# Two FF slices of six chunks moved into the attention stage, with partial sums kept in DRAM

## The chip, the cores and the metric

The kernel runs on one core of one Trainium2 chip. The time is that of one execution in device microseconds. Three runs of the kernel before gave 1572.54, 1577.17 and 1578.33 us, with a median of 1577.17 us.

## The reference

Three layers follow each other, all in float32 (4608 tokens of 512 features):

```python
# 1. attention, 8 batches x 8 heads, 576 queries, 64 features; keys and values pooled by 8 to 72
scores = scale * np.matmul(q, k_p.transpose(0, 1, 3, 2)); attn = softmax(scores); x = attn @ v_p
# 2. gated feed-forward, FF = 1536
g = x @ w_gate; x = (g * sigmoid(g) * (x @ w_val)) @ w_out
# 3. top-1 expert of 8 (width 1024), chosen by logits = x @ w_gate2 + bias[modality]
out[mask] = gate_w[mask, None] * (np.maximum(x[mask] @ w1[e], 0) @ w2[e])
```

## The kernel before

**Stage 1, attention.** 36 tiles of up to 128 queries (`steps`; five per pair of batches hold both heads' halves of a remainder). For a tile x, `st_scores` makes the scores on TensorE and the exponentials on ScalarE, `st_norm` sums and normalises (VectorE and GpSimd), `st_aT` transposes, and `st_av` multiplies by the pooled values and writes x transposed to DRAM (`xT_d`, by a DMA from ScalarE's queue, L313). The pieces are not written in the order of the loop: each is entered with a key by `at_key` (scores of tile x at x-3.0, normalising at x-1.7, transposing at x, and so on; loads and the first weights have keys too) and the pieces are then emitted sorted by key. One key is one tile. The emission order is a priority: a planner, working ahead of the run with durations of its own, fixes the order on each engine, and may take a ready instruction that is emitted somewhat later. At run time each engine, SP's DMA queue among them, works through its own list strictly in order.

**Splits.** All products of stages 2 and 3 are made from two rounded halves (hi, lo), three matmuls for each product: hi·hi, hi·lo and lo·hi. `w_split` makes the halves of one weight part (gate, value or out of one FF slice of 128; three parts a slice): one ScalarE pass, four VectorE passes (L137 to L142), one copy and one subtraction (L149, L150). Weights come as 64-bit numbers, so each part is a DMA of 512 KB (`w_load`). The parts of the first two slices (0 to 5) have keys 21 to 33.5 in the attention; the others follow during stage 2. `x_load` reads one chunk of x (384 tokens) in four pieces through two buffers (`xr`), and splits each (L186 on ScalarE, L187 on VectorE); chunks 0 and 1 have keys 27 and 30.

**Stage 2, feed-forward.** 12 chunks of 384 tokens, 12 slices each: an item (c, f) is `gemm1` (24 matmuls 128x384, line L372, then tanh and products on ScalarE and VectorE) and `gemm2` (9 matmuls 128x512, L394, which add into three PSUM banks over all 12 slices of the chunk). The items of chunks 0 and 1 alternate for as long as weights are split, then chunks 2 to 11 run one after the other. At the end of a chunk `evac` (L403, ScalarE) takes the sums into `row` tiles; `logits` and `gates` (queued in `todo`, one for each item) make the choice of expert, and the rows go to DRAM (`x2_d`).

**Stage 3, experts**, in blocks of 256 gathered tokens: `e_gemm1` (12 matmuls 128x256, L665) and `e_gemm2` (6 matmuls 128x512, L684) for each of 8 slices. The change does not touch it except for the order in which token tiles are numbered.

PSUM has eight banks in one pool for the whole kernel: tag s 2 (`st_av`, `gemm1`), tag x 4 (scores, then sums), tag y 2 (transposes, then sums). `gemm1` of chunk 0 therefore shares its two banks with `st_av`.

Of the kernel before, what the change touches and what calls it, by code (L numbers as in the profile page):

```python
# [44 lines left out]
def const_array():  # L45
    import numpy as np

    p = np.arange(128)
    parts = {"ident": np.eye(128)}
    vm = np.zeros((128, 4, 2, 2))  # L50
    for r in range(H * KEYS):
        c, row, h = r // 128, r % 128, r // KEYS
        vm[row, h // 2, c - h // 2, h % 2] = 1.0 / 8
    parts["vmask"] = vm.reshape(128, 16)
    parts["idhi"] = np.tile(np.arange(TILES) * 1.0, (128, 1))
# [11 lines left out]
def attention_moe_moe2(ctx: ExitStack, tc: tile.TileContext, q, k, v, w_gate, w_val, w_out,  # L67
# [8 lines left out]
    psp = ctx.enter_context(tc.tile_pool(name="psp", bufs=1, space=PSUM))  # L76

    def bank(tag, name):
        return psp.tile([128, 512], F32, tag=tag, bufs={"s": 2, "x": 4, "y": 2}[tag], name=name)

    xT_d = [dram.tile([128, 4, 2 * S], F32, name=f"xT{g}") for g in range(4)]
    x2_d = dram.tile([NT + 1, DM + 1], F32, name="x2d")


    ncst = sum(w for _, w in CONST_W)
# [66 lines left out]
    def load_bias(p0):  # L152
        t0 = m1.tile([128, 2, CH], F32, tag="xh", bufs=4, name="biast").rearrange("p a n -> p (a n)")
        mraw = t0[:TILES, 0:256].bitcast(I32).rearrange("i (p w) -> i p w", w=2)
        mf = t0[:TILES, 256:384]
        m = t0[:, 384:420]
        z = t0[:, 420:456]
        tmp = t0[:, 456:744].rearrange("p (t e) -> p t e", e=E)
        bb = t0[:, 744:760].rearrange("p (m e) -> p m e", e=E)
        sy.dma_start(out=mraw.rearrange("i p w -> i (p w)"),  # L160
                     in_=modality.bitcast(I32).rearrange("(i x) -> i x", i=TILES))
        sy.dma_start(out=bb.rearrange("p m e -> p (m e)"),
                     in_=mbias.rearrange("m e -> (m e)").partition_broadcast(128))
        ve.tensor_copy(mf, mraw[:, :, 0])
        mps = bank("s", "mps")
# [24 lines left out]
        xc[c] = (hi, lo)  # L190


    w2p = [None]
    with tc.tile_pool(name="p0", bufs=1) as p0:
# [52 lines left out]
        def st_scores(x):  # L247
            b, i = steps[x]
            e = e_t[x % NE]
            nm = p0.tile([128, 8], F32, tag="nm", bufs=4, name="nm")  # L250
            for j in range(2):
                sc = bank("x", "sc")
                for hp in (2 * j, 2 * j + 1):
                    dst = sc[:, (hp % 2) * 144:(hp % 2) * 144 + 144]
                    if i < 4:
                        pe.matmul(dst, lhsT=q_t[b][:, hp, i * 128:(i + 1) * 128],
                                  rhs=kb_t[b % 2][:, hp].rearrange("p r k -> p (r k)"), start=True, stop=True)
                    else:
# [24 lines left out]
        def st_aT(x):  # L283
# [4 lines left out]
            else:  # L288
                views = [(b + w, 1, slice(64 * w, 64 * w + 64), slice(256, 320)) for w in range(2)]
            for c0, cn in ((0, 4), (4, 1)):  # L290
                ap = bank("y", "aTp")[:, 0:cn * 128].rearrange("p (c n) -> p c n", c=cn)
                for c in range(cn):
                    pe.transpose(ap[:, c, :], e[:, (c0 + c) * 128:(c0 + c + 1) * 128], ident)
                for bb, half, ss, cs in views:
                    o = at_tile(bb, half)[:, c0:c0 + cn, cs]
                    if cn == 1 or x % 2:
                        ve.tensor_copy(o, ap[:, :, ss])  # L297
                    else:
                        ac.copy(o, ap[:, :, ss])

        def st_av(b, half, hp):
# [16 lines left out]
            ev_.append((key, len(ev_), fn, args))  # L318

        as_, an, av, avs = 3.0, 1.7, 0.7, 0.45  # L320
        for x in range(len(steps)):
            at_key(x - as_, st_scores, x)
            at_key(x - an, st_norm, x)
# [61 lines left out]
    def gemm2(c, f):  # L385
        hh, hl = h_t.pop((c, f))
        w = wo[f // 2]
        if f == 0:
            x2ps[c] = [bank("xxy"[tt], "x2") for tt in range(CT)]
        for tt in range(CT):  # L390
            o = x2ps[c][tt]
            ts = slice(tt * 128, (tt + 1) * 128)
            for n, (a, hx) in enumerate(((0, hh), (1, hh), (0, hl))):
                pe.matmul(o, lhsT=hx[:, ts], rhs=w[:, f % 2, a, :], start=f == 0 and n == 0,  # L394
                          stop=f == NF - 1 and n == 2)

    rows_t, small = {}, {}

    def evac(c):
        rows = []  # L400
        for tt in range(CT):
            r = m1.tile([128, DM + 1], F32, tag="row", bufs=3, name="row")
            ac.activation(out=r[:, 0:DM], in_=x2ps[c][tt], func=ACTF.Copy, scale=0.5)  # L403
            rows.append(r)
        rows_t[c] = rows
# [420 lines left out]
```

## Time and profile before

| | us |
|---|---|
| median of three runs | 1577.17 |
| the profiled execution's own time | 1575.83 |
| its span (first to last instruction) | 1574.1 |
| stage 1: start to the first `gemm1` matmul (L372) | 192.3 |
| stage 2: from there to its last matmul, some | 907 |
| TensorE busy over the span | 1505.1 (96%) |
| VectorE, ScalarE, GpSimd busy | 949.3, 617.1, 194.5 |

The profile names engines PE (TensorE), PEld (its weight loads), DVE (VectorE), ACT (ScalarE), POOL (GpSimd) and SP. A wait is told by the engine that idles and the instruction that ended the wait. Matmuls are pipelined, so a duration in a row overlaps the next one; the pace is read from the starts.

### The profile page before, as it was taken

Reading aid. Unit: us, or ns where it says so; the run is one execution under the profiler, and the core shown is the slowest. Engines: PE = TensorE matmul, PEld = TensorE weight load, DVE = VectorE, ACT = ScalarE, POOL = GpSimd, SP = SyncE. Lnnn points to the kernel's source line nnn. Section 1 sums busy time; section 2 is a strip of 40 time slices with the busy share of each in tenths; the row PEclk is TensorE's granted clock in tenths of the full one; section 3 lists DMA queues with packets and bytes.
Section 4 is the critical chain, followed back from the end, with each engine's and each line's share of the span. In section 5 each row is a group of like instructions: output and inputs, shape, how many; then the busy total and the mean of one; then the engine's idle time right before and its main releaser. Section 6 shows DMA issues by size and latency. Waiting matters only on the chain.

```text
span 1574.1 us, 22647 instructions
## 1 busy us (share of the span) xinstructions
PE 1505.1 (96%) x8472; PEld 1367.7 (87%) x8472; DVE 949.3 (60%) x2252; ACT 617.1 (39%) x1385; POOL 194.5 (12%) x201
## 2 busy tenths in 40 slices
PE   5778899999999999999999999999999999999996
PEld 4566699999999999999999999998889889898985
DVE  5677799555555564637272727277986666666660
ACT  4567555432222121212121212123556656666661
POOL 4866300000000000000000000001031111211101
PEclk8998999999999999999999999999999999999998
DMA  7775534210000000000010100007477666666520
GB/s 287 291 268 187 184 139 161 67 31 30 11 30 31 11 31 31 11 30 24 17 41 1 40 1 31 1 21 265 141 231 258 224 229 223 218 225 224 191 98 28
DMA packets 47816, 179.58 MB, mean 114 GB/s; under 512 B 5421, under 2 KB 19921, under 8 KB 34898
## 3 DMA queue, kind: packets, MB, share of 16 engines
q1 hardware_dynamic: 33170, 149.19, 26.9%
q0 software_dynamic: 6080, 19.42, 3.5%
q10 hardware_dynamic: 8448, 9.44, 1.7%
q8 instruction: 68, 1.11, 0.3%
q14 instruction: 50, 0.41, 0.1%
HBM read 149.70 MB, written 28.86 MB: 113 GB/s over the span
## 4 chain that ended last, share of the span: by engine, by line
PE 85%; DVE 4%; issue 4%; POOL 4%; DMA 2%; ACT 1%; POOLq 0%; SPq 0%; ACTq 0%
PE gv L372 38%; PE x L394 19%; PE hp L665 12%; PE po L684 12%; PE xp L308 2%; POOL vraw L232 1%; PE tp L649 1%; POOL e L276 1%; DVE kp L222 1%; DMA x2d<-row 1%; ACT e L267 1%; DVE sm L273 1%; DVE at L297 0%; POOL vb L238 0%; DVE nm L263 0%
## 5 line engine op out<-in xcount | busy, mean ns | idle before, releaser
L372 PE MATMUL gv<-xh,gv 128*128 128x384 f32 x2304 | 611.3, 336 | 0.2 <-DVE t L377 0.2
L372 PEld LDWEIGHTS gv<-xh,gv 128*128 128x128 f32 x2304 | 421.1, 188 | 6.8 <-DVE t L377 0.6
L372 PE MATMUL gv<-xl,gv 128*128 128x384 f32 x1152 | 390.4, 339 | 0.0
L394 PE MATMUL x<-wo,hh 128*128 128x512 f32 x864 | 273.4, 398 | 0.0
L665 PEld LDWEIGHTS hp<-x2hl,w 128*128 128x128 f32 x1824 | 234.1, 189 | 10.9
L665 PE MATMUL hp<-x2hl,w 128*128 128x256 f32 x1824 | 243.1, 282 | 0.0
L372 PEld LDWEIGHTS gv<-xl,gv 128*128 128x128 f32 x1152 | 216.3, 188 | 5.9
L377 DVE SCALAR_TENSOR_TENSOR t<-t,gv 128x384 f32<-128x384 f32 x144 | 79.6, 552 | 233.1 <-ACT t L376 232.6
L376 ACT ACTIVATE t<-gv 128x384 f32<-128x384 f32 x144 | 70.7, 491 | 327.0 <-PE gv L372 326.7
L684 PE MATMUL po<-w,hh 128*128 128x512 f32 x608 | 193.4, 400 | 3.1 <-ACT hh L669 3.1
L414 DVE CUSTOM_DVE_ANT_0 junk<-row,w2g 128x512 bf16<-128x512 f32 x288 | 184.8, 684 | 3.6 <-ACT row L403 3.5
L394 PEld LDWEIGHTS x<-wo,hh 128*128 128x128 f32 x864 | 161.6, 189 | 27.0
L636 DVE TENSOR_TENSOR w<-raw,w 128x512 fp32r<-128x512 f32 x152 | 106.1, 698 | 116.8 <-ACT w L634 116.6
L381 ACT CAST hh<-t 128x384 fp32r<-128x384 f32 x144 | 73.8, 513 | 258.6 <-DVE t L378 258.4
L394 PE MATMUL x<-wo,hl 128*128 128x512 f32 x432 | 171.2, 396 | 0.0
L559 POOL DMA_INDIRECT xg<-x2d,gidx x38 | 38.3, 1007 | 1052.0 <-DVE oidx L546 913.2
L634 ACT CAST w<-raw 128x512 fp32r<-128x512 f32 x152 | 94.0, 619 | 135.4 <-PE po L684 124.8
L378 DVE TENSOR_TENSOR t<-t,gv 128x384 f32<-128x384 f32 x144 | 79.3, 551 | 74.3 <-PE gv L372 74.1
L684 PE MATMUL po<-w,hl 128*128 128x512 f32 x304 | 121.4, 399 | 0.0
L684 PEld LDWEIGHTS po<-w,hh 128*128 128x128 f32 x608 | 103.7, 188 | 17.6 <-ACT hh L669 3.3
L382 DVE TENSOR_TENSOR hl<-t,hh 128x384 fp32r<-128x384 f32 x144 | 80.1, 556 | 51.8 <-ACT hh L381 51.5
L638 DVE TENSOR_TENSOR w<-raw,w 128x512 fp32r<-128x512 f32 x152 | 103.7, 682 | 0.0
(127 smaller groups left out, 1468.8 us busy)
## 6 DMA issues: line engine op xcount, KB each, us to landing
raw<-in_moe_w_dram SPq DMA_DIRECT2D x76, 1024.0 KB, 4.9
vraw<-in_v_dram SPq DMA_DIRECT2D x8, 1280.0 KB, 12.0
x2d<-row SPq DMA_DIRECT2D x36, 256.5 KB, 3.7
kraw<-in_k_dram SPq DMA_DIRECT2D x8, 1152.0 KB, 8.8
qt<-in_q_dram SPq DMA_DIRECT2D x8, 1152.0 KB, 7.0
xr<-xT SPq DMA_DIRECT2D x48, 192.0 KB, 2.4
w2g<-in_moe_w_gate_dram SPq DMA_DIRECT2D x12, 512.0 KB, 3.6
w2g<-in_moe_w_val_dram SPq DMA_DIRECT2D x12, 512.0 KB, 3.5
```

The lines of the kernel that those rows point to most:

```text
L372: pe.matmul(p, lhsT=w[:, a, ws], rhs=x[kk], start=n == 0, stop=n == 11)
L377: ve.scalar_tensor_tensor(out=t, in0=t, scalar=1.0, in1=o[0], op0=ALU.add, op1=ALU.mult)
L378: ve.tensor_tensor(out=t, in0=t, in1=o[1], op=ALU.mult)
L381: ac.copy(hh, t)
L382: ve.tensor_tensor(out=hl, in0=t, in1=hh.bitcast(F32), op=ALU.subtract)
L394: pe.matmul(o, lhsT=hx[:, ts], rhs=w[:, f % 2, a, :], start=f == 0 and n == 0, stop=f == NF - 1 and n == 2)
L414: ve.tensor_tensor_reduce(out=junk, in0=r[:, 0:DM], in1=w2g[:, e, :], scale=1.0, scalar=0.0, op0=ALU.mult, op1=ALU.add, accum_out=L[:, tt, ...
L634: ac.copy(h1, src)
L636: ve.tensor_tensor(out=w[:, 1, 0:512].rearrange("p (k f) -> p k f", k=4), in0=src, in1=h1.bitcast(F32), op=ALU.subtract)
L638: ve.tensor_tensor(out=w[:, 1, 512:1024], in0=w2s, in1=w[:, 0, 512:1024].bitcast(F32), op=ALU.subtract)
L665: pe.matmul(hp, lhsT=w[:, a, c0:c0 + 128], rhs=x[:, kk, :], start=n == 0, stop=n == 11)
L684: pe.matmul(b["po"][tt], lhsT=hx[:, ts], rhs=w[:, a, 512:1024], start=f == 0 and n == 0, stop=f == 7 and n == 2)
```

## The change

Tokens 0 to 2303 (chunks 0 to 5) are also cut into nine units of 256 tokens. FF slices 0 and 1 of these units are computed during stage 1: `u_load` (x of a unit, split), `u_gemm1` (24 matmuls 128x256 and the products) and `u_gemm2` (6 matmuls 128x512), entered with keys 7 to 33.85, one item (u, f) every 1.5 keys. The sums of both slices of a unit go through `row` tiles to DRAM (`part_d`). In stage 2 chunks 6 and 7 come first, with all 12 slices, then chunks 0 to 5 with slices 2 to 11 only, then 8 to 11. `new_rows` loads the partial sums of a chunk, and `evac` adds them on VectorE instead of copying on ScalarE. The splits of weight parts 0 to 5 move from keys 21 to 33.5 to keys 1 to 6, their loads likewise. Stage 1 has a PSUM pool of its own: scores 2 banks (4 before), transposes 2, `st_av` and `u_gemm1` together 2, unit sums 2.

```diff
+EC, EF = 6, 2
+NU = EC * CT // 2
+ORDER = [EC, EC + 1] + list(range(EC)) + list(range(EC + 2, NCH))
+POS = {c: i for i, c in enumerate(ORDER)}
...
-        return psp.tile([128, 512], F32, tag=tag, bufs={"s": 2, "x": 4, "y": 2}[tag], name=name)
+        n = {"s": 2, "x": 4, "y": 2, "sc": 2, "at": 2, "xg": 2, "acc": 2}[tag]
+        return psp[0].tile([128, 512], F32, tag=tag, bufs=n, name=name)
...
+    part_d = [dram.tile([CH, DM], F32, name=f"part{c}") for c in range(EC)]
...
+    def u_load(u):
+        hi, lo = [], []
+        for k2 in range(2):
+            th = m1.tile([128, 2, CH], F32R, tag="xh", bufs=4, name="uh")
+            tl = m1.tile([128, 2, CH], F32R, tag="xl", bufs=4, name="ul")
+            for j in range(2):
+                raw = m1.tile([128, CH], F32, tag="xr", bufs=2, name="ur")[:, 0:256]
...
+                    sy.dma_start(out=raw, in_=xT_d[g0][:, 2 * k2 + j, c0:c0 + 256])
...
+                ac.copy(h, raw)
+                ve.tensor_tensor(out=l, in0=raw, in1=h.bitcast(F32), op=ALU.subtract)
...
+    def u_gemm1(u, f):
+        hi, lo = ue[u]["x"]
+        w = wgv[f]
+        p = bank("xg", "ugv")
+        o = [p[:, 0:256], p[:, 256:512]]
...
+                    pe.matmul(o[j], lhsT=w[:, a, ws], rhs=x[kk], start=n == 0, stop=n == 11)
...
+        ac.activation(out=t, in_=o[0], func=ACTF.Tanh, scale=0.5)
+        ve.scalar_tensor_tensor(out=t, in0=t, scalar=1.0, in1=o[0], op0=ALU.add, op1=ALU.mult)
+        ve.tensor_tensor(out=t, in0=t, in1=o[1], op=ALU.mult)
...
+        ac.copy(hh, t)
+        ve.tensor_tensor(out=hl, in0=t, in1=hh.bitcast(F32), op=ALU.subtract)
...
+    def u_gemm2(u, f):
...
+            ue[u]["acc"] = [bank("acc", "acc") for _ in range(2)]
+        for tt in range(2):
+            for n, (a, hx) in enumerate(((0, hh), (1, hh), (0, hl))):
+                pe.matmul(ue[u]["acc"][tt], lhsT=hx[:, ts], rhs=w[:, f % 2, a, :], start=f == 0 and n == 0,
+                          stop=f == EF - 1 and n == 2)
+        if f == EF - 1:
+            for tt in range(2):
+                r = m1.tile([128, DM + 1], F32, tag="row", bufs=3, name="urow")[:, 0:DM]
+                ac.activation(out=r, in_=ue[u]["acc"][tt], func=ACTF.Copy, scale=0.5)
+                ac.dma_start(out=part_d[c][y * 128:(y + 1) * 128, :], in_=r)
...
-                sc = bank("x", "sc")
+                sc = bank("sc", "sc")
...
-            xp = bank("s", "xp")
+            xp = bank("xg", "xp")
...
+        WS0, WSK, U0, UK = 1.0, 1.0, 7.0, 1.5
-                at_key(12.0 + n, w_load, n)
-                at_key(21.0 + (n - 4) * 2.5 + 0.1, w_load, n)
+            at_key(WS0 - 2.5 + n * 0.5 if n < 4 else WS0 + (n - 4) * WSK + 0.1, w_load, n)
-            at_key(21.0 + n * 2.5, w_split, n)
+            at_key(WS0 + n * WSK, w_split, n)
+        uitems = [(u, f) for u in range(NU) for f in range(EF)]
+        for n, (u, f) in enumerate(uitems):
+            x = U0 + n * UK
+            if f == 0:
+                at_key(x - 3.0, u_load, u)
+            at_key(x, u_gemm1, u, f)
+            at_key(x + 0.9 * UK, u_gemm2, u, f)
-        at_key(5.0, load_bias, p0)
-        at_key(27.0, x_load, 0)
-        at_key(30.0, x_load, 1)
+        at_key(3.5, load_bias, p0)
+        at_key(31.0, x_load, ORDER[0])
+        at_key(34.5, x_load, ORDER[1])
...
+    psp[0] = ctx.enter_context(tc.tile_pool(name="psp", bufs=1, space=PSUM, reuse_waits="tile"))
...
+    def new_rows(c):
...
+                sy.dma_start(out=rows_t[c][tt][:, 0:DM], in_=part_d[c][tt * 128:(tt + 1) * 128, :])
...
     def evac(c):
...
+            if c < EC:
+                ve.scalar_tensor_tensor(out=r, in0=x2ps[c][tt], scalar=0.5, in1=r, op0=ALU.mult, op1=ALU.add)
+            else:
+                ac.activation(out=r, in_=x2ps[c][tt], func=ACTF.Copy, scale=0.5)
...
-    for c in range(2, NCH):
-        items += [(c, f) for f in range(NF)]
+    for c in ORDER[2:]:
+        items += [(c, f) for f in range(EF if c < EC else 0, NF)]
```

## Rows read from the trace of the kernel before

**Rows 1.** The page: span, and busy time of each engine
```profile
span 1574.1 us, 22647 instructions
PE 1505.1 (96%) x8472; PEld 1367.7 (87%) x8472; DVE 949.3 (60%) x2252; ACT 617.1 (39%) x1385; POOL 194.5 (12%) x201
```

**Rows 2.** Stretch, length; busy PE, PEld, DVE, ACT, POOL; PEclk, DMA share, GB/s
```profile
0.00:20.00 20.00, 8.33 (x37) 7.72 (x37) 9.99 (x17) 8.88 (x30) 3.56 (x15) 0.95 0.91 371
20.00:55.00 35.00, 25.36 (x126) 19.88 (x126) 21.07 (x47) 18.12 (x71) 27.00 (x26) 0.83 0.63 252
55.00:192.30 137.30, 110.94 (x597) 87.36 (x595) 103.70 (x211) 88.08 (x311) 83.86 (x85) 0.93 0.60 217
192.30:341.90 149.60, 149.39 (x785) 139.51 (x784) 110.56 (x222) 72.31 (x123) 0.00 (x0) 1.00 0.33 115
341.90:1099.10 757.20, 755.23 (x3989) 704.76 (x3987) 409.08 (x1136) 163.97 (x331) 3.09 (x3) 1.00 0.10 33
```

**Rows 3.** PE's waits up to 200 us: total, times, longest
```profile
PE aTp L293 <- POOL e L276: 28.3, 15, 4.4
PE xp L308 <- ACT xs L310: 5.5, 3, 2.4
```

**Rows 4.** PE in order of time: the first `gemm1` matmul of two neighbouring items
```profile
1003.16 0.34 PE L372 MATMUL gv<-xh,gv 128*128 128x384 f32 x1
...
1009.46 0.34 PE L372 MATMUL gv<-xh,gv 128*128 128x384 f32 x1
```

**Rows 5.** PE in order of time: one slice of an expert block
```profile
1301.19 1.57 PE L665 MATMUL hp<-x2hl,w 128*128 128x256 f32 x12
1302.59 0.63 PE L684 MATMUL po<-w,hh 128*128 128x512 f32 x2
...
1304.01 1.57 PE L665 MATMUL hp<-x2hl,w 128*128 128x256 f32 x12
```

**Rows 6.** Groups of DVE instructions by line and shape, 0 to 192.3 us
```profile
L140 DVE SCALAR_TENSOR_TENSOR wa<-w2g,wa 128x512 int32<-128x512 int32 x9 | 8.7, 962 | 0.2
L142 DVE SCALAR_TENSOR_TENSOR wa<-w2g,wa 128x512 int32<-128x512 int32 x9 | 7.4, 826 | 0.1
L138 DVE TENSOR_SCALAR wa<-wa 128x512 int32<-128x512 int32 x9 | 5.3, 590 | 0.1
L137 DVE TENSOR_SCALAR wa<-wa 128x512 f32<-128x512 f32 x9 | 4.9, 541 | 0.4 <-ACT wa L136 0.4
L150 DVE TENSOR_TENSOR gv<-wa,gv 128x512 fp32r<-128x512 f32 x4 | 4.5, 1128 | 0.0
L150 DVE TENSOR_TENSOR wo<-wa,wo 128x512 fp32r<-128x512 f32 x2 | 1.4, 680 | 0.0
```

**Rows 7.** The same view, 192.3 to 340 us
```profile
L140 DVE SCALAR_TENSOR_TENSOR wa<-w2g,wa 128x512 int32<-128x512 int32 x27 | 18.4, 683 | 0.0
```

**Rows 8.** Groups of ACT instructions, 1100 to 1574 us
```profile
L669 ACT ACTIVATE hh<-hp 128x256 fp32r<-128x256 f32 x152 | 58.4, 384 | 52.7 <-PE hp L665 52.7
L403 ACT ACTIVATE row<-x 128x512 f32<-128x512 f32 x3 | 1.8, 599 | 0.6 <-PE x L394 0.4
```

**Rows 9.** Groups of DVE instructions, 1100 to 1574 us
```profile
L670 DVE SCALAR_TENSOR_TENSOR hl<-hp,hh 128x256 fp32r<-128x256 f32 x152 | 63.4, 417 | 20.6 <-ACT hh L669 20.3
L652 DVE TENSOR_TENSOR x2hl<-tp,x2hl 128x512 fp32r<-128x512 f32 x38 | 25.8, 680 | 1.7 <-ACT x2hl L651 1.7
```

**Rows 10.** DMA issues up to 200 us: count, KB, us to landing
```profile
xT<-xs ACTq DMA_DIRECT2D x8, 640.0 KB, 6.2
xr<-xT SPq DMA_DIRECT2D x10, 192.0 KB, 2.7
```

**Rows 11.** In order of time: the tail of one `x_load`, and a DMA issue on ACT
```profile
172.91 0.51 ACT L186 CAST xh<-xr 128x384 fp32r<-128x384 f32 x1 [3.12 <-DMA xr<-xT]
...
175.40 2.50 PE L308 MATMUL xp<-at,vb 128*128 128x320 f32 x4 [2.37 <-ACT xs L310]
...
180.50 0.52 ACTq L313 DMA_DIRECT2D xT<-xs  x1
```

More of the change, by code (lines that the diff above doesn't have):

```diff
@@ L54, in const_array @@
     parts["vmask"] = vm.reshape(128, 16)
-    parts["idhi"] = np.tile(np.arange(TILES) * 1.0, (128, 1))
+    parts["idhi"] = np.tile(np.array([c * CT + t for c in ORDER for t in range(CT)]) * 1.0, (128, 1))
     parts["idlo"] = np.tile(p[:, None] + 1.0, (1, TILES))
@@ L75, in attention_moe_moe2 @@
     m1 = ctx.enter_context(tc.tile_pool(name="m1", bufs=1))
-    psp = ctx.enter_context(tc.tile_pool(name="psp", bufs=1, space=PSUM))
+    psp = [None]
     def bank(tag, name):
-        return psp.tile([128, 512], F32, tag=tag, bufs={"s": 2, "x": 4, "y": 2}[tag], name=name)
+        n = {"s": 2, "x": 4, "y": 2, "sc": 2, "at": 2, "xg": 2, "acc": 2}[tag]
+        return psp[0].tile([128, 512], F32, tag=tag, bufs=n, name=name)
     xT_d = [dram.tile([128, 4, 2 * S], F32, name=f"xT{g}") for g in range(4)]
     x2_d = dram.tile([NT + 1, DM + 1], F32, name="x2d")
+    part_d = [dram.tile([CH, DM], F32, name=f"part{c}") for c in range(EC)]
     ncst = sum(w for _, w in CONST_W)
@@ L164, in load_bias @@
         ve.tensor_copy(mf, mraw[:, :, 0])
-        mps = bank("s", "mps")
+        mps = bank("xg", "mps")
         pe.transpose(mps[:, :TILES], mf, ident[:TILES, :TILES])
@@ L190, in x_load @@
         xc[c] = (hi, lo)
+    ue = {}
+    def u_load(u):
[5 more added lines that the diff above has]
+                raw = m1.tile([128, CH], F32, tag="xr", bufs=2, name="ur")[:, 0:256]
+                g0, g1 = 2 * u // 9, (2 * u + 1) // 9
+                c0 = (2 * u % 9) * 128
+                if g0 == g1:
+                    sy.dma_start(out=raw, in_=xT_d[g0][:, 2 * k2 + j, c0:c0 + 256])
+                else:
+                    sy.dma_start(out=raw[:, 0:128], in_=xT_d[g0][:, 2 * k2 + j, c0:c0 + 128])
+                    sy.dma_start(out=raw[:, 128:256], in_=xT_d[g1][:, 2 * k2 + j, 0:128])
+                h, l = th[:, j, 0:256], tl[:, j, 0:256]
+                ac.copy(h, raw)
+                ve.tensor_tensor(out=l, in0=raw, in1=h.bitcast(F32), op=ALU.subtract)
+                hi.append(h)
+                lo.append(l)
+        ue[u] = {"x": (hi, lo)}
@@ new lines, in u_gemm1 @@
+    def u_gemm1(u, f):
[3 more added lines that the diff above has]
+        o = [p[:, 0:256], p[:, 256:512]]
+        for j in range(2):
+            n = 0
+            for kk in range(4):
+                ws = slice(j * 512 + kk * 128, j * 512 + (kk + 1) * 128)
+                for a, x in ((0, hi), (0, lo), (1, hi)):
+                    pe.matmul(o[j], lhsT=w[:, a, ws], rhs=x[kk], start=n == 0, stop=n == 11)
+                    n += 1
+        t = m1.tile([128, CH], F32, tag="t", bufs=2, name="ut")[:, 0:256]
+        ac.activation(out=t, in_=o[0], func=ACTF.Tanh, scale=0.5)
+        ve.scalar_tensor_tensor(out=t, in0=t, scalar=1.0, in1=o[0], op0=ALU.add, op1=ALU.mult)
+        ve.tensor_tensor(out=t, in0=t, in1=o[1], op=ALU.mult)
+        hh = m1.tile([128, CH], F32R, tag="hh", bufs=2, name="uhh")[:, 0:256]
+        hl = m1.tile([128, CH], F32R, tag="hl", bufs=2, name="uhl")[:, 0:256]
+        ac.copy(hh, t)
+        ve.tensor_tensor(out=hl, in0=t, in1=hh.bitcast(F32), op=ALU.subtract)
+        ue[u][f] = (hh, hl)
@@ new lines, in u_gemm2 @@
+    def u_gemm2(u, f):
+        hh, hl = ue[u].pop(f)
+        w = wo[f // 2]
+        if f == 0:
+            ue[u]["acc"] = [bank("acc", "acc") for _ in range(2)]
+        for tt in range(2):
+            ts = slice(tt * 128, (tt + 1) * 128)
+            for n, (a, hx) in enumerate(((0, hh), (1, hh), (0, hl))):
[5 more added lines that the diff above has]
+                ac.activation(out=r, in_=ue[u]["acc"][tt], func=ACTF.Copy, scale=0.5)
+                c, y = divmod(2 * u + tt, CT)
+                ac.dma_start(out=part_d[c][y * 128:(y + 1) * 128, :], in_=r)
+            del ue[u]
@@ L193, in attention_moe_moe2 @@
     w2p = [None]
-    with tc.tile_pool(name="p0", bufs=1) as p0:
+    with tc.tile_pool(name="p0", bufs=1) as p0, tc.tile_pool(name="ps0", bufs=1, space=PSUM) as ps0:
+        psp[0] = ps0
         NE = 4
@@ L290, in st_aT @@
             for c0, cn in ((0, 4), (4, 1)):
-                ap = bank("y", "aTp")[:, 0:cn * 128].rearrange("p (c n) -> p c n", c=cn)
+                ap = bank("at", "aTp")[:, 0:cn * 128].rearrange("p (c n) -> p c n", c=cn)
                 for c in range(cn):
@@ L339, in attention_moe_moe2 @@
         for n in range(3 * NW1 + 4):
-            if n < 4:
-                at_key(12.0 + n, w_load, n)
-            else:
-                at_key(21.0 + (n - 4) * 2.5 + 0.1, w_load, n)
+            at_key(WS0 - 2.5 + n * 0.5 if n < 4 else WS0 + (n - 4) * WSK + 0.1, w_load, n)
         for n in range(3 * NW1):
-            at_key(21.0 + n * 2.5, w_split, n)
-        at_key(5.0, load_bias, p0)
-        at_key(27.0, x_load, 0)
-        at_key(30.0, x_load, 1)
+            at_key(WS0 + n * WSK, w_split, n)
+        uitems = [(u, f) for u in range(NU) for f in range(EF)]
+        for n, (u, f) in enumerate(uitems):
+            x = U0 + n * UK
+            if f == 0:
+                at_key(x - 3.0, u_load, u)
[4 more added lines that the diff above has]
+        at_key(34.5, x_load, ORDER[1])
         for key, _, fn, args in sorted(ev_, key=lambda t: t[:2]):
@@ L387, in gemm2 @@
         w = wo[f // 2]
-        if f == 0:
+        f0 = EF if c < EC else 0
+        if f == f0:
             x2ps[c] = [bank("xxy"[tt], "x2") for tt in range(CT)]
@@ L393, in gemm2 @@
             for n, (a, hx) in enumerate(((0, hh), (1, hh), (0, hl))):
-                pe.matmul(o, lhsT=hx[:, ts], rhs=w[:, f % 2, a, :], start=f == 0 and n == 0,
+                pe.matmul(o, lhsT=hx[:, ts], rhs=w[:, f % 2, a, :], start=f == f0 and n == 0,
                           stop=f == NF - 1 and n == 2)
     rows_t, small = {}, {}
+    def new_rows(c):
+        if c in rows_t:
+            return
+        rows_t[c] = [m1.tile([128, DM + 1], F32, tag="row", bufs=3, name="row") for tt in range(CT)]
+        if c < EC:
+            for tt in range(CT):
+                sy.dma_start(out=rows_t[c][tt][:, 0:DM], in_=part_d[c][tt * 128:(tt + 1) * 128, :])
     def evac(c):
-        rows = []
+        if c not in rows_t:
+            new_rows(c)
         for tt in range(CT):
[L402 to L405, printed above, removed]
+            r = rows_t[c][tt][:, 0:DM]
+            if c < EC:
+                ve.scalar_tensor_tensor(out=r, in0=x2ps[c][tt], scalar=0.5, in1=r, op0=ALU.mult, op1=ALU.add)
+            else:
+                ac.activation(out=r, in_=x2ps[c][tt], func=ACTF.Copy, scale=0.5)
     def logits(c, tt, es):
@@ L419, in gates @@
         rows = rows_t.pop(c)
-        ti = slice(c * CT, (c + 1) * CT)
+        ti = slice(POS[c] * CT, (POS[c] + 1) * CT)
         bc = [128, CT, E]
-        ve.tensor_tensor(out=L, in0=L, in1=biasall[:, ti, :], op=ALU.add)
+        ve.tensor_tensor(out=L, in0=L, in1=biasall[:, c * CT:(c + 1) * CT, :], op=ALU.add)
         mx = m1.tile([128, CT], F32, tag="mx", bufs=2, name="mx")
@@ L434, in gates @@
         for tt in range(CT):
-            i = c * CT + tt
+            i = POS[c] * CT + tt
             ve.tensor_tensor(out=CU[:, i + 1, :], in0=CU[:, i, :], in1=OH[:, i, :], op=ALU.add)
@@ L738, in attention_moe_moe2 @@
     keys1 = [(1, j) for j in range(J1)] + [(2, j) for j in range(J2MIN)]
-    items = [(c, f) for f in range(NF - 2) for c in range(2)]
-    items += [(c, f) for c in range(2) for f in range(NF - 2, NF)]
-    for c in range(2, NCH):
-        items += [(c, f) for f in range(NF)]
+    items = [(c, f) for f in range(NF - 2) for c in ORDER[:2]]
+    items += [(c, f) for c in ORDER[:2] for f in range(NF - 2, NF)]
+    for c in ORDER[2:]:
+        items += [(c, f) for f in range(EF if c < EC else 0, NF)]
     prev = None
@@ L746, in attention_moe_moe2 @@
         gemm1(c, f)
-        if c == 0:
+        if c == ORDER[0]:
             w_feed(3)
@@ L755, in attention_moe_moe2 @@
                 todo.append((gates, cc_))
+                nx = ORDER[POS[cc_] + 1]
+                if POS[cc_] and nx < EC:
+                    todo.append((new_rows, nx))
                 if cc_ == NCH - 2:
@@ L759, in attention_moe_moe2 @@
         prev = (c, f)
-        if f == NF - 1 and c + 2 < NCH:
-            x_load(c + 2)
+        if f == NF - 1 and POS[c] + 2 < NCH:
+            x_load(ORDER[POS[c] + 2])
         if todo:
-            do_todo(2 if c == NCH - 1 else 1)
+            do_todo(2 if c == NCH - 1 or len(todo) > 8 and c < EC else 1)
     gemm2(*prev)
```

## The prediction

> **What bounds the kernel now.** I first read the page's busy times [rows 1]: TensorE is busy for 96% of the span, so a change can win only where TensorE idles or where its work becomes less. Where it idles is told by the table of busy time by stretch [rows 2]. From 192.3 to 1099.1 us, all of stage 2, PE is busy for 904.6 of 906.8 us at full clock: nothing is to be had there except by taking matmuls away. The three stretches before it make up stage 1. There PE is idle for 11.7, 9.6 and 26.4 us, 47.7 us in all, and the granted clock is 0.95, 0.83 and 0.93. No other engine is near its limit over the whole stage: DVE is busy 134.8 of 192.3 us, ACT 115.1, POOL 114.4. Then I asked what PE waits for [rows 3]: 28.3 us in 15 waits for the normalised exponentials from POOL, 5.5 us for the copies out of the `st_av` banks on ACT. So stage 1 is a set of loosely coupled in-order engines in which PE has little else to do while a chain runs; more matmuls that are ready could fill these holes. The profiled execution took 1575.83 us for a span of 1574.1 us. The sum below is made against it; the median of the three runs is 1.3 us higher, and the forecast is moved by that at the end.
>
> **The matmuls removed and added.** One item of stage 2 takes 6.30 us, from the start of one `gemm1` to the next [rows 4], and 144 of them are 907 us, which is the whole stage, so items follow each other without a hole. Six chunks lose two slices: 12 x 6.30 = 75.6 us leave a full PE. In the experts the same shapes as in a unit follow each other [rows 5]: 12 matmuls 128x256 in 1.40 us, then 6 of 128x512 in 1.42 us. A unit's item has 24 and 6: 2.80 + 1.42 = 4.22 us, and 18 items are 76.0 us. PE's work is thus not made less (+0.4 us). All that can be won is idle time and slow clock of stage 1, and the ledger of stage 1 is the prediction.
>
> **The early splits.** Six splits move from keys 21 to 33.5 to keys 1 to 6, which lie in the stretch 20 to 55 us. Their DVE time in stage 1 is 0.54 + 0.59 + 0.96 + 0.83 us and for the subtraction 5.9 us over 6, 0.98 us: 3.90 us each, 23.4 us for six [rows 6]. DVE is idle in that stretch for 35 - 21.1 = 13.9 us [rows 2]. Packed without a hole this makes the stretch 9.5 us longer; with none of it covered, 23.4 us. DVE at 90% gives (21.1 + 23.4) / 0.9 = 49.4 us, 14 us longer. I take 13 us, nearer to the dense packing, because the planner may place ready splits ahead of waiting instructions. PE has no units to fill this time except what it can take up early: a unit needs its x from DRAM, and `st_av`'s DMAs land 6.2 us after issue and the reads 2.7 us [rows 10]. I credit one item, 4 us, between none and two (8.4 us).
>
> The row for the first pass shows 0.96 us in stage 1 and 0.68 us when POOL is silent [rows 6, 7], so splits and POOL already hinder each other. The Trainium skill, "SBUF — State Buffer", section "Who interferes with whom", says that a VectorE instruction with two SBUF inputs and a GpSimd instruction that reads SBUF take one port, and that the later one waits for the whole of the other. The rows agree in direction. By that rule the early place is worse, since POOL is busy for 77% of 20 to 55 us against 61% of the stretch after it: the 1.0 us of excess per split (3.90 against 2.89 us outside) would become some 1.3 us as an estimate, and the sum below would be 1.6 us higher.
>
> **The fill.** After the splits stage 1 has one item each 1.5 keys. What the units put on ACT is 36 pieces of x and 36 passes of tanh and copy at 0.384 us, 18 sums at 0.60 us [rows 8] and 18 DMA issues of 0.52 us [rows 11]: 27.6 + 10.8 + 9.4 = 47.8 us. On DVE it is 36 + 54 passes at 0.417 us [rows 9], 37.5 us. With a stage of 258 us this makes DVE 67%, ACT 63%, POOL 44%, and PE some 84% over the whole and about 94% after the splits. So PE is the engine that sets the pace there, with the exponentials made well ahead of need. Of the 26.4 us of idle time in 55 to 192.3 us I take 16 us as filled; the bounds are none and all of it. I stop at 16 because PE gets two new causes to wait: `st_av` and the units share two banks, and a `u_load` reads its four pieces through two buffers, so ACT waits in line for the third. That wait is seen in the trace for `x_load`: 3.12 us on ACT, 2.37 us on PE behind the copies of `st_av` [rows 11].
>
> The clock of 55 to 192.3 us is 0.93 [rows 2], that is 9.6 us of it lost in clock, about half of this if the slow level is half speed and PE works all the time. With fewer holes I take 3 us back, between 0 and 5. The Trainium skill, "TensorE: Matmul & The Clock Gate", section "What's actually happening", says that the clock follows how busy the engine has been of late; no row here contradicts it, and if it held for every hole the sum would be 2 us lower.
>
> **What follows in stage 2.** `evac` of six chunks goes from ACT (0.60 us) to DVE, 18 x 0.68 us by the nearest subtraction out of PSUM [rows 8, 9]. DVE is 54% busy there [rows 2], so I cost it at nothing as long as PE has both `gemm1` banks ahead; without that cover `evac` (2.0 us) stands before the products of the next item, at most 2 us a chunk, 12 us. I take 1 us in all. The loads of partial sums are queued on SP after `gates`, by their place in `todo` before the chunk's last items, and behind the rows' own writes; nothing waits for them unless SP is held by an `x_load`, which is two chunks ahead. The four loads of weights that now come before key 1 are 2 MB, at 371 GB/s [rows 2] 5.6 us of DMA in front of the next keys and values; they find the second stretch at a share of 0.63. I take 0, and at most 5.6 us. What was at keys 21 to 33.5 leaves DVE 23 us freer late in stage 1; that is in the fill.
>
> **Sum.** +76.0 - 75.6 + 13 - 4 - 16 - 3 + 1 = -8.6 us: stage 1 ends at about 258 us instead of 192.3 us, and stage 2 is 75 us shorter. 1575.8 - 8.6 = 1567.2 us; with 1.3 us for the median, 1568.5 us, -0.55%. Own range of this case: 1560 to 1577 us.
>
> **Rivals.**
>
> *The holes fill entirely.* If all 26.4 us are filled, the early stretch costs its dense 9.5 us, two items run in it (-8.4) and the clock gives 5 us, the sum is 0.4 + 9.5 - 8.4 - 26.4 - 5 + 1 = -29 us, 1548 us. For it: no engine but PE is over 67%. Against it: all are in order, and the 28.3 us [rows 3] are short waits, at most 4.4 us, which a list fixed ahead does not meet exactly; half-way there is 1555 to 1560 us. 0.22.
>
> *Loads of units stall ACT, and PE with it (slower).* The mechanism is the third piece of each `u_load`. Nine loads at the measured 2.37 us on PE are 21 us, less what the forecast's remaining idle time already holds (10.4 us at most). With the same fill elsewhere the sum is -8.6 + 21 = +12.4 us, 1590 us; it turns from faster to slower where each load costs PE over 1 us. For it: one such wait in the trace, and loads of keys and values that share the queue (DMA share 0.60). Against it: of two `x_load`s in stage 1 only one shows it, and with units PE has other matmuls. 0.18.
>
> *The units do not run between the tiles.* The planner could place them behind the attention, for want of banks or `row` tiles. Then 76.0 - 75.6 + 13 + 1 = +14 us, 1592 us. Against it: their keys end at 33.85, before the last tiles. 0.05.
>
> *The early stretch takes back all that the fill gives.* With 23.4 us uncovered and the rest as forecast, the sum is +1.8 us, 1579 us, no change. For it: DVE is saturated and POOL is at 77% there. 0.13.
>
> The forecast itself has 0.42.
>
> **How the numbers follow.** A change of less than 0.5%, 7.9 us, can hardly be told from none here. The forecast's case lies across that bound, a little more than half of it beyond: 0.23 faster, 0.17 same, 0.02 slower. The full fill gives 0.22 faster. The early stretch gives 0.03 faster, 0.07 same, 0.03 slower, the stalls 0.02, 0.04 and 0.12, the units behind the attention 0.05 slower. Together 0.50 faster, 0.28 same, 0.22 slower. The range reaches from short of the full fill's end to the stalled case: 1547 to 1588 us.
>
> **What would show it.** The table by stretch of the changed kernel: unit matmuls (128x256) between some 60 and 240 us and PE at 90% or more there; DVE saturated before, with the splits between 20 and 70 us; the first 128x384 matmul near 258 us; the period of items still 6.30 us afterwards, with no hole at the ends of chunks. Waits of ACT for pieces of x, and of PE for ACT behind them, above 15 us in all would show the slower rival. A first 128x384 matmul before 245 us, or after 268 us, makes the forecast wrong.

## The result, and the profile after

The changed kernel took 1562.15 us (median) against 1577.17 us: the ratio is 0.9911, 95% interval 0.9892 to 0.9929. One of its five runs took 2482.42 us at a granted clock of 0.56 and is left out of the ratio; the other four took 1561.88 to 1563.90 us. The forecast was 1568.5 us, faster, within 1547 to 1588 us. The profiled execution took 1562.15 us, 13.7 us less than that of before.

From the page of the changed kernel, the span and the engines' busy times [rows 1]:

```profile
span 1560.4 us, 23227 instructions
PE 1501.4 (96%) x8616; PEld 1364.2 (87%) x8616; DVE 980.9 (63%) x2324; ACT 630.7 (40%) x1433; POOL 199.2 (13%) x201
```

The busy time by stretch of the changed kernel, columns as in [rows 2]; the borders are now the first unit matmul (65.2 us) and the first 128x384 matmul of stage 2 (253.5 us):

```profile
0.00:20.00 20.00, 7.47 (x28) 6.80 (x29) 9.54 (x15) 7.72 (x25) 3.56 (x15) 1.00 0.92 374
20.00:65.20 45.20, 30.99 (x148) 23.08 (x146) 38.53 (x78) 27.02 (x91) 28.21 (x24) 0.77 0.67 243
65.20:253.50 188.30, 177.94 (x1126) 152.26 (x1125) 126.64 (x268) 116.21 (x385) 85.02 (x87) 0.99 0.56 196
253.50:403.10 149.60, 149.08 (x783) 139.40 (x782) 112.20 (x226) 72.34 (x123) 0.00 (x0) 1.00 0.35 116
403.10:1086.60 683.50, 680.77 (x3595) 635.37 (x3593) 399.28 (x1118) 141.73 (x289) 3.10 (x3) 1.00 0.13 44
```

Stage 1 ends 61.2 us later. In its long stretch PE is busy for 94.5% at a clock of 0.99, where it was 81% at 0.93; in the stretch before it the clock fell from 0.83 to 0.77. PE's idle time in stage 1 is 12.5 + 14.2 + 10.4 = 37.1 us after 47.7 us before; its busy time grew by 71.8 us for 76.0 us of new matmuls. The lines of `gemm1` tell stage 2: count, durations, then the first and the last start (kernel before, then after):

```profile
L372 PE MATMUL gv<-xh,gv x2304: 332/337/577, 192.3 to 1096.8; 128*128 128x384 f32 x192
```

```profile
L450 PE MATMUL gv<-xh,gv x2112: 334/337/580, 253.5 to 1084.3; 128*128 128x384 f32 x192
```

From 904.5 to 830.8 us it is 73.7 us shorter. So +61.2 - 73.7 = -12.5 us, and the remaining 1.2 us lie in stage 3, whose length differed by 2.2 us among all kernels below and is not explained.

PE's waits up to 270 us in the changed kernel (total, times, longest), as [rows 3]; the waits for POOL have gone from 28.3 to 8.1 us and the new ones, for the units' own products (`acc`) and the shared banks (`xp` for `ut`), are small:

```profile
PE aTp L365 <- POOL e L348: 8.1, 6, 4.0
PE mps L173 <- DVE biast L171: 3.7, 1, 3.7
PE acc L253 <- ACT uhh L241: 2.8, 1, 2.8
PE acc L253 <- DVE uhl L242: 2.6, 4, 1.0
PE xp L380 <- DVE ut L238: 2.5, 3, 1.3
PE xp L380 <- ACT xs L382: 1.5, 3, 0.8
```

### The profile page after: what moved, and what is told of

It reads as the page before. It is cut to its first block, busy times and chain, and to the rows that moved or that the text cites. A ratio compares the mean times of both kernels' runs of the same rounds, so it can differ in the third digit from the quotient of the medians.

```text
span 1560.4 us, 23227 instructions
## 1 busy us (share of the span) xinstructions
PE 1501.4 (96%) x8616; PEld 1364.2 (87%) x8616; DVE 980.9 (63%) x2324; ACT 630.7 (40%) x1433; POOL 199.2 (13%) x201
## 5 line engine op out<-in xcount | busy, mean ns | idle before, releaser
L450 PE MATMUL gv<-xh,gv 128*128 128x384 f32 x2112 | 563.6, 338 | 1.3 <-DVE t L455 1.3
L450 PEld LDWEIGHTS gv<-xh,gv 128*128 128x128 f32 x2112 | 385.0, 188 | 7.7 <-DVE t L455 2.1
L450 PE MATMUL gv<-xl,gv 128*128 128x384 f32 x1056 | 356.6, 338 | 0.0
L473 PE MATMUL x<-wo,hh 128*128 128x512 f32 x792 | 249.8, 396 | 0.0
L450 PEld LDWEIGHTS gv<-xl,gv 128*128 128x128 f32 x1056 | 198.4, 188 | 5.3
L455 DVE SCALAR_TENSOR_TENSOR t<-t,gv 128x384 f32<-128x384 f32 x132 | 73.1, 553 | 190.3 <-ACT t L454 189.9
L473 PEld LDWEIGHTS x<-wo,hh 128*128 128x128 f32 x792 | 147.9, 189 | 24.3
L473 PE MATMUL x<-wo,hl 128*128 128x512 f32 x396 | 157.1, 397 | 0.0
L456 DVE TENSOR_TENSOR t<-t,gv 128x384 f32<-128x384 f32 x132 | 72.9, 552 | 61.7 <-PE gv L450 61.5
L460 DVE TENSOR_TENSOR hl<-t,hh 128x384 fp32r<-128x384 f32 x132 | 73.4, 556 | 42.1 <-ACT hh L459 42.0
```

What stands on the lines that cost most here:

```text
L450: pe.matmul(p, lhsT=w[:, a, ws], rhs=x[kk], start=n == 0, stop=n == 11)
L455: ve.scalar_tensor_tensor(out=t, in0=t, scalar=1.0, in1=o[0], op0=ALU.add, op1=ALU.mult)
L456: ve.tensor_tensor(out=t, in0=t, in1=o[1], op=ALU.mult)
L460: ve.tensor_tensor(out=hl, in0=t, in1=hh.bitcast(F32), op=ALU.subtract)
```

## The experiments

What the kernels win or lose is decided in the main in stage 1, so each run is told by the time of its first 128x384 matmul ("end"), by PE's idle time until then, and by the length of stage 2 from the first to the last of these matmuls; all three are from the profiled execution. That is one run of each kernel: those of e2, e3, e5 and e8 took 2.1 to 3.0 us less than their medians, that of e11 took 3.6 us more. The medians are of runs on the chip; of the kernel before they are 1575.2 to 1578.8 us beside these runs.

| kernel | median us | end | PE idle | stage 2 |
|---|---|---|---|---|
| before | 1577.2 | 192.3 | 47.7 | 904.5 |
| changed | 1562.2 | 253.5 | 37.1 | 830.8 |
| e1 early splits only | 1583.2 | 200.5 | 54.2 | 904.7 |
| e2 units behind the attention | 1584.0 | 267.4 | 45.9 | 834.9 |
| e3 four chunks in units | 1569.8 | 232.9 | 40.7 | 855.3 |
| e4 four raw buffers | 1565.2 | 256.7 | 37.3 | 830.5 |
| e5 eight chunks in units | 1574.4 | 282.0 | 37.6 | 809.3 |
| e6 bias table later | 1567.0 | 257.4 | 37.8 | 830.1 |
| e7 early splits, own PSUM pool, no units | 1588.5 | 203.7 | 53.0 | 904.9 |
| e8 own PSUM pool only | 1572.4 | 187.1 | 45.3 | 904.5 |
| e9 splits without their passes | 1567.3 | 256.9 | 39.1 | 830.3 |
| e10 units one key later | 1572.9 | 262.2 | 42.3 | 830.5 |
| e11 splits 1.5 keys apart | 1562.9 | 256.1 | 37.8 | 831.4 |
| e12 value pooling on VectorE | 1575.1 | 267.6 | 45.4 | 829.6 |

**e1: the early splits alone.**

```diff
-                at_key(12.0 + n, w_load, n)
...
-                at_key(21.0 + (n - 4) * 2.5 + 0.1, w_load, n)
+            at_key(1.0 - 2.5 + n * 0.5 if n < 4 else 1.0 + (n - 4) + 0.1, w_load, n)
...
-            at_key(21.0 + n * 2.5, w_split, n)
-        at_key(5.0, load_bias, p0)
+            at_key(1.0 + n, w_split, n)
+        at_key(3.5, load_bias, p0)
```

> The kernel before with one part of the change alone: the first six weight splits, their loads and the bias at the new early keys, no units. Theory A (the gain is PE's idle time of late stage 1, filled by units): stage 1 gets some 5 to 8 us longer before tile 8 and gets a part of it back later, because DVE has 23 us less there; its end lies between 188 and 198 us (192.3 before) and the time between 1573 and 1583 us. Rival B (the early splits relieve DVE late in stage 1, and that is the gain): stage 1 ends at 182 us or before, the time is 1567 us or less.

Measured: 1583.18 us, ratio 1.0042 (1.0026 to 1.0058). Counted from 0, tile 7 is transposed at 63.0 us (55.1 before), tile 21 at 135.7 (120.0), tile 35 at 194.1 (182.1), and stage 1 ends 8.2 us later. Rival B falls: of the 15.7 us lost by tile 21 some 7.5 us come back late, and no gain is left. Theory A's bounds, 188 to 198 us and 1573 to 1583 us, were missed too, narrowly in the time: I had expected more to come back.

**e2: the same work, nothing between the tiles.**

```diff
-        WS0, WSK, U0, UK = 1.0, 1.0, 7.0, 1.5
+        WS0, WSK, U0, UK = 1.0, 1.0, 43.0, 1.5
...
-        at_key(31.0, x_load, ORDER[0])
-        at_key(34.5, x_load, ORDER[1])
+        at_key(68.0, x_load, ORDER[0])
+        at_key(70.5, x_load, ORDER[1])
```

> The changed kernel with the units' keys moved behind the last tile (43 and later instead of 7 and later; the loads of chunks 6 and 7 behind them). Same work, nothing between the tiles. Theory A: the units cost their full 76 us after the attention, stage 1 ends 270 us or later, and the gain is gone: 1580 to 1597 us. Rival B: the gain stays, 1567 us or less. Also: if the two-input DVE passes of the units (664 and 645 ns between the tiles) are slow because of POOL, they take about 420 ns here, where POOL is silent.

Measured: 1583.96 us, ratio 1.0047 (1.0034 to 1.0061). The units' first and last matmuls, the changed kernel's and then those of e2, and the busy time of e2 while its units run (columns as in [rows 2]):

```profile
L233 PE MATMUL ugv<-uh,gv x288: 276/281/388, 65.2 to 238.7; 128*128 128x256 f32 x144
```

```profile
L233 PE MATMUL ugv<-uh,gv x288: 274/282/523, 187.1 to 263.1; 128*128 128x256 f32 x144
187.00:267.20 80.20, 79.29 (x542) 71.94 (x541) 37.05 (x89) 37.55 (x89) 0.52 (x1) 1.00 0.39 124
```

In e2 the units take 80 us for 76.0 us of matmuls, and POOL is all but silent (0.52 us). To stand between the tiles is thus worth 21.8 us to the changed kernel by the medians and 19.6 us by the spans: 13.9 us at the end of stage 1, 4.1 us in stage 2, and 1.6 us after it. In stage 2 PE waits 4.1 us for `t`; 3.7 us of it stand behind a weight split on DVE and ACT, for which ACT, by the trace, waits 4.1 us until the last partial sums are written. The end came earlier than the 270 us expected. The groups of DVE passes up to 267 us, the changed kernel's first, then those of e2, tell the price of POOL:

```profile
L218 DVE TENSOR_TENSOR ul<-ur,uh 128x256 fp32r<-128x256 f32 x36 | 23.4, 664 | 11.2 <-ACT uh L217 11.1
L242 DVE TENSOR_TENSOR uhl<-ut,uhh 128x256 fp32r<-128x256 f32 x18 | 11.6, 645 | 0.6 <-ACT uhh L241 0.3
L238 DVE TENSOR_TENSOR ut<-ut,ugv 128x256 f32<-128x256 f32 x18 | 7.5, 416 | 0.3
```

```profile
L218 DVE TENSOR_TENSOR ul<-ur,uh 128x256 fp32r<-128x256 f32 x36 | 15.5, 443 | 12.0 <-ACT uh L217 11.9
L242 DVE TENSOR_TENSOR uhl<-ut,uhh 128x256 fp32r<-128x256 f32 x18 | 7.6, 424 | 5.8 <-ACT uhh L241 5.7
L238 DVE TENSOR_TENSOR ut<-ut,ugv 128x256 f32<-128x256 f32 x18 | 7.6, 421 | 0.6
```

The two passes that read both operands from SBUF take 664 and 645 ns between the tiles and 443 and 424 ns where POOL is silent; the one that reads an operand from PSUM takes the same in both.

**e3 and e5: fewer and more units.** The edits are `EC, EF = 4, 2`, and `EC, EF = 8, 2` with `UK = 1.13`, which puts the items closer together.

> The changed kernel with four chunks instead of six in units (six units, 12 items, keys 7 to 25; chunks 4 and 5 first afterwards). Theory A: the idle time is filled only while units last, two thirds of the 16 us, and the early cost of 5 us stays: 7 to 11 us under the kernel before instead of 15, 1566 to 1571 us. Rival B (early splits) and any gain from the separate PSUM pool or from the order of chunks: the same time as with six, 1560 to 1564 us.

> The changed kernel with eight chunks in units (24 items, one each 1.13 keys; chunks 8 and 9 first afterwards). Theory A: with six chunks PE idles only 10.4 us after the splits, so the matmuls of two more chunks find no room; they only change places: 1556 to 1566 us, within some 6 us of the changed kernel. Rival (the gain is in proportion to the units: 1569.8 with four and 1562.2 with six): 1555 us or less.

Measured: 1569.76 us, ratio 0.9957 (0.9944 to 0.9971), and 1574.41 us, 0.9993 (0.9982 to 1.0005). With e7 as the stage 1 without units, 12, 18 and 24 items lengthen it by 29.2, 49.8 and 78.3 us for 50.6, 76.0 and 101.3 us of matmuls: 21.4, 26.2 and 23.0 us are filled or won by the clock. e3 came as expected. The last two chunks of eight add 28.5 us to stage 1 and take 21.5 us from stage 2, so in the one order tried they win nothing beyond six; a difference of 3 us between such sums is no more than one execution makes, so where exactly the hole is full is not shown. The forecast for e5 was missed: I had expected these matmuls to change places at no cost. They lose 3.2 us in stage 1, and in stage 2 they give 3.7 us less than the 25.2 us of the four items that leave it. Of these, 2.3 us are waits of PE for `t`, 3.6 us in e5 and 1.3 us in the changed kernel.

**e7 and e8: the PSUM pool by itself**, since the attention of e2 ended at 187 us, 13 us before stage 1 of e1.

```diff
-                sc = bank("x", "sc")
+                sc = bank("sc", "sc")
...
-            xp = bank("s", "xp")
+            xp = bank("xg", "xp")
```

> The early splits as in e1, and stage 1 with a PSUM pool of its own (scores 2 banks, transposes 2, st_av 2) as in the change, no units. In e1 stage 1 ended at 200.4 us, in e2 the attention ended at 187.0 us with the same early splits. Theory D (the pool of its own frees the seam: gemm1 and the next splits no longer hang on st_av's banks): 185 to 191 us, time 1566 to 1574 us. Theory E (the difference is the two loads of x for the first chunks, which e2 had put behind the attention): 197 to 203 us, 1579 to 1586 us.

> The kernel before with the PSUM pool of its own alone (scores with 2 banks instead of 4). Theory D: stage 1 ends 8 us or more earlier, at 184 us or before, time 1569 us or less. Theory E: no change, 190 to 195 us, 1574 to 1581 us; with two score banks rather than four it could also be up to 3 us longer.

Measured: 1588.5 us, ratio 1.0089 (1.0071 to 1.0106), and 1572.44 us, 0.9989 (0.9976 to 1.0001). Theory D falls: with early splits the pool makes stage 1 3.2 us longer, without them 5.2 us shorter. It has no worth of its own that could be added. Theory E's bounds were missed as well, 203.7 us against 197 to 203 and 187.1 us against 190 to 195. Why the attention of e2 ends at 187 us is left open; the loads of x for the first two chunks and the splits of later weights, which e7 has in it and e2 has behind, were not tried apart.

**e4: no wait for a unit's third piece.**

```diff
-                raw = m1.tile([128, CH], F32, tag="xr", bufs=2, name="ur")[:, 0:256]
+                raw = p0q[0].tile([128, 256], F32, tag="ur", bufs=4, name="ur")
```

> The changed kernel with four buffers instead of two for the raw pieces of a unit, so that no piece waits for an earlier one to be split. Theory A: ACT's 7.3 us of waits for pieces reach PE hardly at all, since PE idles only 10.4 us after the splits and not for these; within 3 us of the changed kernel, 1559 to 1565 us. Rival C (unit loads stall ACT and PE behind it): 6 us or more faster, 1556 us or less.

Measured: 1565.21 us, ratio 0.9929 (0.9915 to 0.9942); the edge of theory A's range, and not faster. Rival C, which was the prediction's slower rival, is not borne out: ACT's waits for the pieces fall from 7.3 us to 2.9 us and the time does not. Before the same passes ACT now waits longer for PE (14.9 us instead of 6.9 us), so its idle time there did not become less.

**e6, e9 and e11: is it DVE that makes the early stretch long?** e6 moves `load_bias` to key 20 and gives it a tile of its own; e9 leaves out the four VectorE passes L144 to L149 of the first six splits; e11 sets `WSK` to 1.5.

> The changed kernel with the bias table (load_bias, some 4.7 us of DVE and a transposition for which PE waits 3.7 us) at key 20 instead of 3.5, in a tile of its own. Theory A (the early stretch, 20 to 65 us, is bound by DVE, and what DVE gains there PE gains): first unit matmul 3 to 6 us earlier, time 1556 to 1559.5 us. Rival (PE's wait there is only moved, the chain through POOL sets the pace of the first tiles): 1561 to 1564 us.

> The changed kernel with the four VectorE passes that rebuild a weight from its 64-bit form left out for weight parts 0 to 5 (the splits in the early stretch lose some 2.6 of 3.3 us each, 15 to 16 us of DVE in all; the values of slices 0 and 1 differ). Theory A (the early stretch is bound by DVE because of the splits, and what it loses is lost to the end): tile 7 at 55 to 57 us instead of 62.7, the first unit 5 us or more earlier, stage 1 ends 4 to 9 us earlier, 1553 to 1558 us. Rival (an earlier tile 7 is used up later, as when the bias table was moved): stage 1 ends within 3 us of 253.5 us, 1560 to 1565 us.

> The changed kernel with the six splits 1.5 keys apart (keys 1 to 8.5) instead of one, which still has each before its first use in units. Theory A (DVE of the early stretch is what is dear): tile 7 at 58 to 61 us, 1558 to 1562 us, a version a little faster than the change. Rival (order alone): 1562 us or more.

Measured: 1567.01 us, ratio 0.9947 (0.9930 to 0.9965); 1567.33 us, 0.9945 (0.9925 to 0.9965), of which e9's stage 1 alone may be compared, because with other values other experts are chosen; 1562.91 us, 0.9907 (0.9886 to 0.9928), the same as the changed kernel. A part of what theory A said came about: in e6 the first unit matmul comes at 59.3 us instead of 65.2, and in e9 tile 7 at 53.4 us instead of 62.7. Neither kernel has both: in e6 tile 7 comes at 64.2 us (what e9's rival says of e6 took tile 6, at 50.2 us, for tile 7), and in e9 the first unit matmul comes at 68.8 us. Stage 1 ends at 257.4 and 256.9 us, no earlier than in the changed kernel. The rivals, which had 1561 to 1564 us for e6 and an end within 3 us of 253.5 us for e9, were missed narrowly too. In e11 tile 7 comes at 63.4 us, where theory A had 58 to 61, and the time is its rival's. The stretch from 20 to 65 us, the changed kernel's first, then e9's:

```profile
20.00:65.00 45.00, 30.79 (x145) 22.88 (x144) 38.33 (x78) 26.83 (x91) 28.09 (x23) 0.77 0.67 242
```

```profile
20.00:65.00 45.00, 29.57 (x133) 22.23 (x133) 29.69 (x62) 26.62 (x91) 28.49 (x28) 0.75 0.55 203
```

DVE has 8.6 us less to do, and PE does not do more. In e9 PE waits 4.0 us for POOL at 59.7 us, whose pooling of the second batch's values runs from 48.9 to 58.5 us in e9 and from 49.0 to 57.8 us in the changed kernel. Which chain is the last there was not settled. That it is not the splits' DVE time alone is what e9 shows, in the one order that it has.

**e10: the same kernel, one key later.**

```diff
-        WS0, WSK, U0, UK = 1.0, 1.0, 7.0, 1.5
+        WS0, WSK, U0, UK = 1.0, 1.0, 8.0, 1.5
```

> The changed kernel with all units one key later (8.0 instead of 7.0). No term of the ledger changes except that a unit's work stands one tile later; any difference beyond 2 us is what another order on the engines makes by itself. Theory A: 1560 to 1566 us. If the changed kernel's order is a lucky one among its neighbours, 1566 us or more.

Measured: 1572.87 us, ratio 0.9980 (0.9966 to 0.9994). No term of the ledger has changed, and 10.7 us are gone, so theory A is missed and the changed kernel's order is a lucky one among its neighbours: +8.7 us in stage 1, of which 5.2 us are idle time of PE and 3.5 us busy time at a lower granted clock (0.97 instead of 0.99 after 65 us). The longest new wait is in one place. The rows of e10 in order of time, of POOL, DVE and PE:

```profile
112.61 4.55 POOL L304 TENSOR_TENSOR vraw<-vraw 128x1280 f32<-128x1280 f32 x2 [0.47 <-DMA vraw<-in_v_dram]
```

```profile
113.14 4.30 DVE L218 TENSOR_TENSOR ul<-ur,uh 128x256 fp32r<-128x256 f32 x2
117.36 0.41 DVE L237 SCALAR_TENSOR_TENSOR ut<-ut,ugv 128x256 f32<-128x256 f32 x1
```

```profile
118.25 1.94 PE L380 MATMUL xp<-at,vb 128*128 128x320 f32 x3 [6.96 <-DVE at L369]
```

Two `ul` passes, 0.76 us together when POOL is silent, took 4.30 us and ended 0.3 us after POOL's two additions; the copy of a transposed tile stood behind them on DVE, and PE, which works through its list in order, idled for 7.0 us. The Trainium skill, "SBUF — State Buffer", section "Who interferes with whom", says that of a GpSimd and a VectorE instruction that both want the shared port the later one stands still until the other is through. These rows agree.

**e12: POOL's long additions taken away.**

```diff
-            for w in (4, 2, 1):
-                o = t[:, :, 0:w] if w > 1 else vs_t[b % 2].unsqueeze(2)
-                gp.tensor_tensor(out=o, in0=t[:, :, 0:w], in1=t[:, :, w:2 * w], op=ALU.add)
+            ve.tensor_reduce(out=vs_t[b % 2], in_=t.rearrange("p c r d -> p c d r"), op=ALU.add, axis=AX.X)
```

> The changed kernel with the pooling of the values (three POOL additions a batch, up to 2.9 us each) done by one reduction on VectorE, which has one SBUF input. Theory F (VectorE's passes with two SBUF inputs stand still while POOL runs such an addition, and PE behind them; in e10 two ul passes of 128x256 took 4.30 us beside a POOL pass of 4.55 us and PE waited 7.0 us): the mean of ul and uhl falls from 664 and 645 ns to 550 or less although DVE has 8 x some 2.8 us more to do, PE's waits for POOL fall under 4 us, stage 1 ends at 252 us or before, 1553 to 1561 us. Rival G (DVE's own load sets the pace of stage 1): +22 us on DVE, of which two reductions fall into the early stretch, make it longer; 1563 us or more.

Measured: 1575.1 us, ratio 0.9980 (0.9969 to 0.9991). Groups of DVE passes up to 260 us:

```profile
L302 DVE TENSOR_REDUCE vsum<-vraw 128x320 f32<-128x2560 f32 x8 | 37.2, 4656 | 2.9 <-POOL vb L308 2.9
...
L218 DVE TENSOR_TENSOR ul<-ur,uh 128x256 fp32r<-128x256 f32 x36 | 16.4, 475 | 7.7 <-ACT uh L217 7.7
...
L242 DVE TENSOR_TENSOR uhl<-ut,uhh 128x256 fp32r<-128x256 f32 x18 | 9.4, 520 | 1.6 <-ACT uhh L241 1.5
```

Theory F is right on its mechanism: the passes fall to 475 and 520 ns, PE's waits for POOL to 2.9 us. Rival G is right on the time: the reduction, reading with a stride, takes 4.66 us where I had put 2.8, DVE is busy for 34.7 of the 35 us from 65 us on, and stage 1 gets 14 us longer. No kernel tried beats the changed one; e11 equals it.

## Why the prediction was right, point by point

- **Matmuls removed and added** (-75.6, +76.0 us). Stage 2 is 73.7 us shorter. PE's busy time in stage 1 grew by 71.8 us, 4.2 us less than the matmuls put in. I put this down to the clock, for which 3 us stood in the sum, bounds 0 to 5; it is a difference of busy times and was not measured apart.
- **The fill** (-16 us). PE's idle time after the early stretch fell from 26.4 us to 10.4 us, to a tenth what was put, and for the reason given: the waits for POOL, 19.5 us from 55 us on before, vanish behind units, with none left after 65 us. e2 shows that it is the place of the units that does it. Part of this agreement is luck of the order: of six kernels with the same or a near ledger (changed, e4, e6, e9, e10, e11) stage 1 ends at 253.5 to 262.2 us, 257.1 us in the mean, and the forecast had 258.3 us.
- **The early splits** (+13 us, less 4 us for a unit run early). This term was mis-sized, and its reason is not borne out. PE's idle time before the first unit grew by 5.4 us instead of 9 us (0.9 us before 20 us, 4.6 us after). Tile 7 is indeed 7.6 us later, and by themselves the splits, with their loads and the bias table, cost 8.2 us (e1). DVE was busy for 85% of the stretch. But with 8.6 us less for DVE stage 1 ends no earlier (e9), nor does it with the first unit 5.9 us earlier (e6), so "DVE at 90%" is not shown to set the length once units follow.
- **DVE's prices.** The six splits took 19.6 us, not 23.4: L149 998 ns, L147 660, L144 514, L145 408, L157 677 in the mean, 3.26 us each. By the rule of the Trainium skill, "SBUF — State Buffer", section "Who interferes with whom", they were to become dearer in the early place, by 0.3 us each as an estimate; they became cheaper by 0.6 us. The rule names the passes that are at risk, not how often they meet POOL. Where it did count I had not put it: the units' 54 passes with two SBUF operands were priced at 417 ns by a row whose operand lies in PSUM and took 664 and 645 ns, 13 us of DVE more.
- **Stage 2** (+1 us). It is 1.9 us: PE's waits for `t` are 1.3 us (0.2 before), the rest is below what the trace tells. One of them, 0.74 us at 486 us, stands behind the first `evac` on DVE, which had waited 3.0 us for its partial sums from DRAM; the prediction had put this load at nothing. The other, 0.52 us at 359 us, stands behind ACT's copies of the gate weights, L705.
- **The rivals.** The full fill did not come, and more units did not bring it nearer (e5). The early stretch took back 5.4 us, not all. Taking most of ACT's waits for the pieces away won nothing (e4); the price of that rival, +12.4 us, had also left out the 10.4 us of idle time that its own text subtracts, with which it is +2 us. Units behind the attention would have given +14 us by the ledger and gave +6.8 us (e2), the attention ending 5 us earlier than before.

The sum in one line, forecast and measured: idle before the first unit +9 and +5.4, fill -16 and -16.0, clock -3 and -4.2, matmuls +0.4 with +1 for stage 2 against +0.4 and +1.9, stage 3 nothing and -1.2; -8.6 and -13.7 us.

## What to carry to other kernels

Where one engine is full in one stage and idles in another, moving its work changes no total; what can be won is the idle time of the stage that receives it, less what is needed early so that the work is ready, and both can be read from a table of busy time by stretch. Such a gain is bounded by the hole: here 21.4, 26.2 and 23.0 us were filled by 12, 18 and 24 items, each in one order, and the kernel with 24 was 12 us slower than that with 18. A single order that was fixed ahead is a draw among its neighbours, here of some 9 us at the end of stage 1 and 10.7 us by the medians, as large as the effects of most edits tried, so compare several orders before a small edit is called good or bad.

## What the runs showed of the hardware

- A VectorE pass with two SBUF operands stands still behind a running POOL addition: two passes that take 0.76 us together otherwise took 4.30 us beside 4.55 us of POOL (e10), and 36 such passes took 664 ns in the mean with POOL busy and 443 ns without (changed kernel, e2). A pass with one operand in PSUM took 416 and 421 ns.
- A reduction on VectorE takes 2.53 us for 2304 neighbouring numbers a partition (L294 of the changed kernel) and 4.66 us for 2560 numbers that lie 256 bytes apart (e12).
- PE's granted clock from 65 us to the end of stage 1 was 0.99 in the changed kernel, where PE was busy for 94.5%, and 0.92 before, where it was busy for 80%. From 20 to 65 us it was 0.77 at a busy share of 68%, and 0.87 before at 78%.
